# Gate weights laid over the query and key weights, first activations over the queries' staging buffer, and a new order of steps in a two-layer block

## The chip, the cores and the metric

The kernel runs on one core of a Trainium2 chip. The core has five engines with a queue of instructions each: TensorE (PE in the profile; its weight loads stand apart as PEld), VectorE (DVE), ScalarE (ACT), GpSimd (POOL) and SyncE (SP), which here issues all DMA transfers. The metric is the time of one execution on the device in microseconds (us). Of several executions the median counts.

## The reference

The input x has 2048 rows of 512 values in float32. The block is an attention layer followed by a gated feed-forward layer, each behind a layer norm and with its input added to its output:

```python
h  = x + A_ref(layernorm(x), wqkv, wo)
h2 = h + B_ref(layernorm(h), w_gate, w_up, w_down)
```

`A_ref` has 32 heads of 16 values and a sliding window: a row looks at itself and at the 255 rows before it. `B_ref` is `(sigmoid(x @ w_gate) * (x @ w_up)) @ w_down` with 1376 inner columns.

## The kernel before, in words

**Numbers.** Products that need float32 accuracy are made from float16 pieces: each operand is split into a high and a low half, and three multiplications (high by high, high by low, low by high) are added up in the accumulator (`mm3`, L360, and its like in `do_group` and `do_mix`). So every weight and every activation passes through a scaling (its largest magnitude is found first: `prep`, `do_amax`, `scale`), a copy that gives the high half and a subtraction that gives the low half.

**First half.** The rows are taken in 8 blocks of 256. For a block, `do_ln` normalizes two tiles of 128 rows and transposes them into `xT`; `do_qk` makes queries and keys from the first two thirds of the weight tile `W1`, and `do_v` makes the values from its last third. Queries go through a staging buffer, `sq0` (`sq1` for block 1), and three DMA copies for each of four parts (`do_queries`) into the tile from which scores are made; keys go through memory (`do_keys`). `do_s` (L635) makes scores for the row maxima, which DVE takes; `do_m` hands the maxima, through a transpose, to the query tile; `do_st` (L680) makes the transposed scores, which ACT exponentiates and POOL masks; `do_pv` multiplies them with the values, `do_o` and `do_wo` bring the result back into rows and project it. The step numbers run through the blocks: s0 to s7 belong to block 0, s56 to s63 to block 7.

**Second half.** The first four tiles of rows are taken one by one: `do_ln2` normalizes and transposes them into `X2`, `do_early` and `do_gu` multiply them with gate and up weights. The other tiles go in pairs (`do_pair`, L1000), and `do_group` multiplies a pair with seven products of halves instead of eight, for which sums and differences of weight halves are kept as well (`do_T`, L945, for gate and up; `do_sums`, L1257, for the down weights). For the last four pairs the down product is folded in the same way (`do_mat` makes seven operands A11, S1, S2, A12, S3, S4, A22 and transposes them by DMA; `do_mix` multiplies them; mix0 to mix3). The remaining tiles go through `do_down`.

**Storage.** Tiles live in pools. The pool `qkv` on the left holds `W1`, `sq0`, `xT` and small tiles. Once the last block's queries, keys, values and query copies are done, `open_x2` (L1542) closes it and opens the pool `x2p` in its place with the high and low halves of the gate weights (`Wg`), the first third of the up weights (`W0u`), the sums of the gate weights (`Tg`) and the four tiles of `X2`. `do_T` for the gate weights loads its pieces into rows 8 to 11 of X, which must have been stashed to memory by then (`vacant0`, `vacant1`).

**Order.** Each piece of work is a generator whose `yield`s name a price, the keys that it needs, and buffers that it takes from a ring. The order of the steps is not worked out in the kernel: `TABLE` (L65) lists all 4458 of them, such as `s0.1`, `prep0/a` or `qk0*4`; a letter behind the slash is the engine where there is a choice (a ACT, v DVE, g POOL). `Order.step` (L267) takes the next step of the named piece and emits its instructions. Each engine, and the DMA queue of SP, runs its own instructions in the order of the list and waits by semaphores for the others. The prices in the `yield`s take no part when the kernel runs; only the program that made the list used them.

```python
def step(self, name, choice):
    piece, (costs, needs, *rest) = self.live[name]
    ...
    self.on = {"v": DVE_, "a": ACT_, "g": POOL_}[choice] if choice else next(iter(costs))
    ...
        self.live[name][1] = piece.send(((0.0, self.on), *places))
```

The functions that the change touches, and what calls them:

Of the kernel before, what the change touches and what calls it, by code (L numbers as in the profile page):

```python
# [69 lines left out]
prep2/v warm0 warm5 load_x6 load_x4 prep1 prep2/v ln3 prep1 prep2/g ln3/v warm7 qk4*4 prep1 prep1/v prep1 prep2/v prep3/v prep2/v prep2/g qk4*3 prep3/v  # L70
prep3/a prep2/a prep3/a prep2/a prep2/g prep2/a*2 prep3 qk4 qk5 qk4/a qk5*4 qk4 ln6 qk5*3 ln5 prep2/g fill0 fill2 ln4/g qk5/a prep1/a prep3 warm6 v2*2 qk5
v2*2 prep1 queries2 queries1 queries3*2 queries1 queries3 queries1 queries0 load_x7 queries0*2 queries6 queries7 queries4 amax2 v0 prep1/v v0 prep1 prep1/a
v2/a v0*2 qk3*3 prep1 prep3 ln7 v0/a queries5 amax1 amax0 queries7 queries5 queries4 qk2 qk3*3 qk2 qk3*2 prep3/a amax2/v amax3 queries2 qk3/a qk2*2 qk3 qk2*4
v1*3 fill0 fill1 qk2/v qk2 prep3/v fill0 prep3/g keys0*2 v1 qk7*3 prep3/v qk7 v1/a qk7*2 qk6 amax1/v ln8 amax3/v prep3/a ln5/a qk6 qk7*2 qk6 ln7 ln6 fill2
prep3/g prep3/v prep3/a amax0/a prep3/g qk6*5 warm8 amax4 queries4 keys0 ln9 qk7/v qk7 v3*2 qk6/v qk6 ln4 v3*2 ln4/v ln5/a queries2 amax4/a v3/a ln5/v prep3/a
s0*2 fill2*2 ln6/a s0 s0.0 s0.1 s0.2 s0*2 s0.3 v4 s0.4 s0*2 s1 ln5 s0.5 s0.6 s1 s1.0 s1.1 s0 v4 s0.7 ln10 ln5/a ln6/a s2 v4 s1 queries7 queries6 amax7
queries6 keys1*2 queries5 amax5 amax6 keys0 s1 s2.0 s1.2 v4 s1.3 s1*2 s1.4 s1 s1.5 s1 s1.6 s2 s1.7 fill2 ln6/g amax7/a v4/a qk8 ln7/a s2 s2.1 qk8 s2.2 s2*2
qk8 s2.3 s2.4 s2 qk8*3 s3*2 s2.5 s3 qk8 ln11 qk8 s3.0 s3.1 s3.2 open_work0 s2 qk9 s3 s2.6 s3.3 s2 qk9 s2.7 s3 qk9 s3.4 s3 qk9 s3 qk9 s3 qk8/a qk8 amax5/a
keys1 amax8 qk9 fill1 ln8 qk9*2 s3.5 s3.6 s3.7 qk9/a s4 qk10 s4.0 m0*2 s4*2 qk10 s4.1 s4 s4.2 s4.3 qk10 s4 s4.4 qk9 qk10 s4 s4.5 s5*2 qk10*4 qk11 s5.0 s5.1 m0
keys1 s5 qk11 s5 qk11*2 s4 s5.2 s4 amax6/a qk10/a prep3/a qk10 s5.3 qk11 s4.6 qk11 s5*2 s4.7 qk11 s5.4 s5.5 s6 qk11 s6.0 s5 s6 qk11/a s5 s5.6 st0*2 ln6 s6.1  # L80
s5.7 s6 st0.0 st0.1 s6 st0 ln7/a s6.2 st0 s6 s6.3 s6 st0.2 qk11 prep3/g ln9 ln11 ln7/g st0.3 s6 st0 ln6/a st0 keys2 amax9 keys2 s6.5 s6.6 v5 s6.4 amax8/v
st0.5 s7*2 s6 ln7 s7.0 s7.1 st0.6 s6.7 s7*2 st1 s7.2 s7 st1.0 s7.3 st1 v5 st1.1 s7.4 ln8/v st1 s7*2 st1 s7 st1.2 s7.5 s7.6 st1.3 s8 ln7/a s7.7 st0.4 st1.4
fill1 st0.7 st1*2 s8 s8.0 m1 s8.1 s8 v5 st1.5 s8.2 st1.6 s8 pv0 st2 s8 s8.3 v5 st2.0 m1 s8.4 st1.7 ln8/a st2 s8 s9 st2 s8 pv0 ln8/g st2.1 v5/a st2.2 s8.5 s8.6
s9.0 ln12 ln9/a ln8 st2 s8 st2 st2.3 s9 qk14 s8.7 st2.5 ln10 st2.4 st2 st2.6 st2.7 s9.1 s9*2 s9.2 qk14 s9 st3 qk14 s9.3 pv0/a st3.0 s9.4 st3 s9 queries8 m1
keys2 queries8 qk14 s10 s9.5 st3.1 st3 s9 s10.0 st3 st3.2 qk14 st3.3 s9.6 s9 st3 ln9/a s9.7 s10 st3.4 st3 s10 qk15 st3.5 s10.1 ln9/g s10 qk14 pv0 s10.2 s10.3
st3.6 st4 qk14 s10 st4.0 st4 ln9 qk14 st4.1 st4 qk15 s10 ln13 st3.7 st4.2 s11 st4 pv1 st4 st4.3 qk14/a st4.5 queries9 amax11 o0 pv1 st4.4 ln10/v s10.4 s10.5
s11 s11.0 pv1/a st4 queries8 amax10 queries9*2 s10 s11.1 st5 s11 st4.6 s10.6 s11 qk15 s11.2 st5.0 st4.7 st5 s11 ln10/a s11.3 s11.4 s11 st5 qk15 st5.1 ln10/g
s11 st5.2 s11.5 st5 s11 s11.6 st5 st5.3 s10 s11.7 st5.5 st5 st5.4 qk15*2 s12*2 st6 s10.7 st5.6 st6.0 qk15*2 st6*2 pv2 s12 queries10 m2 pv1 st5.7 m2 ln11/a
qk14 s12.1 s12.0 s12.2 pv2 o1 qk15/a st6.1 st6.2 s12 pv2/a st6 s12 st6 s12 s12.3 m2 st6.3 s12.4 st6.5 st6 s12.5 s13 s12 st6.6 s13.0 st7 queries10 s12 s12.6
st7.0 st7 queries10 s13 s12.7 st7 st7.1 s13 st7.2 s13.1 st7 s13 st7 st7.3 st7.5 s13 st7 s13.2 pv2 st8 s13 s13.3 s13 pv3 queries11 st7.6 s13.4 queries11 st8.0  # L90
ln12 o0/g st6.4 s13.5 st8 s14 queries11 s13.6 st7.4 st6.7 st7.7 o2 st8.1 st8 s13 s14.0 s14 ln14 s13.7 s14.1 st8 s14 pv3 st8.3 st8.2 s14.2 s14 pv3/a st8 s14
st8 s15 s14.3 qk15 s14.4 st8.6 qk12 st8.7 qk12 st9 s14 qk12 s15.0 pv3 st9.0 s14 st9 qk12 st8.4 o1/g o2/g st8.5 s14.5 st9.1 st9 s15 s14.6 qk12 s15 st9 st9.2
keys3 o3 s15.1 s15 s15.2 qk12 st9 st9.3 s15 s15.3 st9.6 s15.4 st9.5 st9.4 st8.8 qk12 s14 st9 s15 s16 st10 s14.7 st9.7 qk13 s15 qk13 s15.5 s16 st10 s16.0 s15
st10.0 s15.6 s16.1 st10 qk13 pv4 st10.1 o3/g st9.8 s16 qk12 st10 s16 s15.7 s16.2 wo0 st10.2 m3 wo1 qk12/a s17 st10 s16 s16.4 m3 pv4 wo1/g s16.3 s17.0 qk12
st10.6 st10.3 wo1/a m3 st10 pv4/v s16 st11 s17 st10.7 wo1/g ln14 s16.5 s16 qk13 st11.0 wo1 s17.1 st11 qk13 s16 s16.6 st11.1 st11 s16.7 s17 qk13 st11.2 s17.2
st11 s17*2 st11.3 st11 s17 s17.3 qk13 s17.4 st11.6 st11 s17.5 s17 keys2 keys3 st11.7 s17.6 qk13 s17 st12 s18*2 s17.7 ln13 st10.5 st10.4 st11.4 st12.0 s18.0
st12 pv5 wo1 st12.1 s18.1 st12 s18*3 st12 pv4 st12.2 s18.2 wo1 o4 st10.8 st11.5 st11.8 wo0/g s18.3 st12.3 s18.4 s18 st12 s18 st12 s18.5 s18 pv5 s18.7 s18.6
# [1631 lines left out]
```

## Time and profile before

| | us |
|---|---|
| median of 3 runs | 768.06 |
| lowest and highest | 763.97, 768.09 |
| profiled execution | 765.89 |
| its span in the trace | 764.0 |
| PE busy | 734.1 |
| DVE busy | 630.1 |
| ACT busy | 442.8 |
| POOL busy | 337.6 |

The span runs from the first to the last instruction that the profile shows; 1.9 us of the profiled execution lie around it. Busy times are sums over the instructions of an engine; multiplications on PE overlap, and their ends are modelled. A row of a group of instructions reads: line, engine, operation, what it writes and reads, shapes, count, then busy time and mean duration in ns, then the engine's idle time just ahead of them and what ended it. In a table by stages, columns are the engines' busy times, the granted clock of PE, the DMA engines' share and their rate. A row of the timeline gives start and duration in us, engine, line, operation and, in brackets, how long the engine was idle before it and what it waited for.

### The profile page before, as it was taken

The page shows a single profiled execution, that of the slowest core. Times are in us where ns is not written, and L with a number is a line of the kernel's source. Part 1 is how long each engine was busy: PE and PEld are TensorE (multiplying, and loading weights), DVE is VectorE, ACT ScalarE, POOL GpSimd, SP SyncE. Part 2 cuts the span into 40 slices and gives each one's busy share as a digit, 9 for nine tenths or more (in the row PEclk, how much of TensorE's full clock was granted, in tenths as well). Part 3 has the DMA queues.
Part 4 walks back from the last instruction along what each step waited for, and adds up shares of the span by engine and source line. Part 5 has one row for each costly group of instructions (what it writes and reads, how often), then busy time and mean ns, then how long its engine had stood idle before and what let it go on. Part 6 is the DMA issues. An engine that isn't in the chain of part 4 may idle for free.

```text
span 764.0 us, 18698 instructions
## 1 busy us (share of the span) xinstructions
PE 734.1 (96%) x6930; PEld 486.5 (64%) x6930; DVE 630.1 (82%) x1887; ACT 442.8 (58%) x770; POOL 337.6 (44%) x418
## 2 busy tenths in 40 slices
PE   3999999999999999999998899999999899999998
PEld 3777777777777677786765444454544654757473
DVE  6989999988779888697879989976999769596752
ACT  5745888787777778787778966621442224122320
POOL 7653557554553545366547611132330326441620
PEclk9999999999999999999999999999999999999999
DMA  9783463665976655366746658532656754645463
GB/s 316 238 263 100 120 151 67 163 145 116 172 149 152 126 89 116 91 81 142 111 98 139 173 135 250 129 64 59 142 144 143 135 104 85 102 114 88 93 101 83
DMA packets 182395, 100.97 MB, mean 132 GB/s; under 512 B 153440, under 2 KB 159584, under 8 KB 182304
## 3 DMA queue, kind: packets, MB, share of 16 engines
q1 hardware_dynamic: 182304, 99.78, 59.7%
q8 instruction: 54, 0.88, 0.5%
q14 instruction: 37, 0.30, 0.2%
HBM read 37.36 MB, written 13.11 MB: 66 GB/s over the span
## 4 chain that ended last, share of the span: by engine, by line
PE 73%; DVE 12%; DMA 7%; ACT 4%; issue 3%; SPq 1%; DVEq 0%; ACTq 0%
PE mmp L363 23%; PE pvp L747 9%; PE sp L1095 8%; PE sp L659 8%; PE stp L1095 5%; PE stp L721 3%; PE stp L711 3%; PE stp L363 2%; PE pvp L1095 2%; PE sp L1367 2%; PE stp L710 2%; PE stp L712 2%; PE stp L1367 1%; PE sp L363 1%; DVE junk L646 1%
## 5 line engine op out<-in xcount | busy, mean ns | idle before, releaser
L646 DVE CUSTOM_DVE_ANT_0 junk<-sp,mask 128x320 bf16<-128x320 f32 (+4 forms) x512 | 215.0, 466 | 32.4 <-PE sp L659 29.4
L688 ACT ACTIVATE pa<-stp,kappa 128x512 f32<-128x512 f32 (+1 forms) x256 | 157.3, 646 | 40.8 <-PE stp L712 35.5
L659 PE MATMUL sp<-SK,SQ 96*128 96x256 f16 (+3 forms) x960 | 127.6, 232 | 2.9 <-DMA SK<-mem 1.2
L1095 PEld LDWEIGHTS <-SQ 128*128 128x128 f16 x756 | 73.8, 98 | 73.0 <-issue 1.6
L363 PE MATMUL mmp<-xT,W 128*128 128x256 f16 x768 | 109.8, 272 | 1.8 <-ACT xT L316 1.6
L688 ACT ACTIVATE pb<-stp,kappa 128x512 f32<-128x512 f32 x128 | 84.7, 686 | 19.9 <-PE stp L721 18.4
L659 PEld LDWEIGHTS <-SQ 96*128 96x128 f16 x960 | 79.1, 97 | 26.3 <-issue 8.6
L694 POOL TENSOR_SCALAR_AFFINE_SELECT pa<-pa 128x1024 f32<-128x1024 f32 x56 | 63.0, 1128 | 34.0 <-ACT pa L688 34.0
L363 PEld LDWEIGHTS <-W 128*128 128x128 f16 x768 | 70.0, 97 | 12.5 <-issue 4.1
L699 POOL TENSOR_SCALAR_AFFINE_SELECT pa<-pa 128x512 f32<-128x512 f32 x64 | 42.8, 669 | 62.6 <-ACT pa L688 60.3
L747 PE MATMUL pvp<-pa,VT 128*17 128x128 f32 (+1 forms) x1408 | 62.5, 307 | 0.0
L711 PE MATMUL stp<-SQ,SK 100*128 100x256 f16 x224 | 59.9, 270 | 0.0
L699 POOL TENSOR_SCALAR_AFFINE_SELECT pb<-pb 128x512 f32<-128x512 f32 x64 | 42.3, 667 | 33.5 <-ACT pb L688 33.4
L712 PE MATMUL stp<-SQ,SK 100*128 100x128 f16 x256 | 55.4, 218 | 0.2 <-ACT pb L688 0.2
L710 PE MATMUL stp<-SQ,SK 100*128 100x128 f16 x224 | 49.3, 220 | 3.6 <-ACT pa L688 2.6
L747 PEld LDWEIGHTS pvp<-pa,VT 128*17 128x17 f32 x1408 | 37.7, 97 | 22.8 <-issue 2.2
L363 PE MATMUL mmp<-WO,oT 128*128 128x512 f16 x192 | 50.6, 379 | 0.9 <-DMA oT<-whl 0.9
L363 PE MATMUL mmp<-W,xT 128*128 128x512 f16 x192 | 49.5, 379 | 0.0
L721 PE MATMUL stp<-SQ,SK 100*128 100x256 f16 x256 | 47.4, 272 | 1.4 <-ACT pa L688 1.3
L363 PE MATMUL mmp<-WD,hT 128*128 128x512 f16 (+1 forms) x204 | 48.6, 379 | 0.0
L363 PEld LDWEIGHTS <-x 128*128 128x128 f16 x288 | 27.9, 98 | 28.7 <-issue 1.8
L646 DVE DVE_READ_ACCUMULATOR2_ANT mq<- 128x1 f32 x512 | 42.5, 83 | 0.0
(371 smaller groups left out, 1471.3 us busy)
## 6 DMA issues: line engine op xcount, KB each, us to landing
SQ<-sq SPq DMA_DIRECT2D x96, 128.0 KB
SK<-mem SPq DMA_DIRECT2D x16, 384.0 KB
chunk<-in_wd_dram SPq DMA_DIRECT2D x20, 256.0 KB
mem<-sk SPq DMA_DIRECT2D x8, 512.0 KB
...
```

What stands on the lines that cost most here:

```text
L363: PE.matmul(ps, a_of(a, k), b_of(b, k), start=(k == 0 and i == 0), stop=(k == n - 1 and i == 2))
L646: V.tensor_tensor_reduce(out=junk[:, c0:], in0=ps[:, c0:], in1=mask[:, c0:], scale=1.0, scalar=-3.0e38, op0=ALU.add, op1=ALU.max, accum_ou ...
L659: PE.matmul(ps[:, col:col + k1 - k0], q, SK[0:96, (2 * a + hf) % 5, 4 * (p % 2) + j, k0:k1], start=True, stop=True)
L688: S.activation(dst, a, AF.Exp, scale=kappa)
L694: G.affine_select(out=f, in_=f, pattern=[[0, 8], [-1, 128]], compare_op=ALU.is_gt, fill=0.0, base=0, channel_multiplier=1)
L699: G.affine_select(out=p, in_=p, pattern=[[0, 4], [1, 128]], compare_op=ALU.is_ge, fill=0.0, base=0, channel_multiplier=-1)
L710: PE.matmul(a[:, 0:128], ks(k0, g, j), qs(b, g, j, 0, 128), start=True, stop=True)
L711: PE.matmul(a[:, 128:384], ks(k0 + 1, g, j), qs(b, g, j, 0, 256), start=True, stop=True)
L712: PE.matmul(a[:, 384:512], ks(k0 + 3, g, j), qs(b, g, j, 128, 256), start=True, stop=True)
L721: PE.matmul(a[:, u, :], ks(k0 + 2, g, j + u), qs(b, g, j + u, 0, 256), start=True, stop=True)
L747: PE.matmul(ps[32 * j:32 * j + 17, u, q0:q1], VT[:, kt % 6, 8 * j + g, :], w[:, j, c:c + q1 - q0], start=first, stop=last, skip_group_chec ...
L1095: PE.matmul(out, x7[p][0][:, kk, MATS[a], ha, :], mv, start=first and i == 0, stop=i == 5, skip_group_check=True)
```

## The change

The query and key parts of `W1` become a tile of the pool `keep`, which lives throughout; the value part becomes a tile of its own, `W1v`, in the old pool. `sq0` moves to `keep` as well. The gate weights' halves are then written over `W1`, and the four tiles of `X2` are laid over `sq0`. `open_x2` opens only `W0u` and `Tg`. Two steps without work are added: `open_wg` says that `W1` is free (all of block 7's query and key products are done), `open_sq` that `sq0` is free (its query copies are done). The steps that used to wait for `open_x2` wait for the one that concerns them: loads and halves of the gate weights for the first, the normalized rows of `do_ln2` for the second. The folded gate weights, which lie in `Tg`, still wait for `open_x2`.

Some prices are altered, and `TABLE` is replaced as a whole; it has 4460 steps. The number and shapes of the products on PE stay. Some steps change their engine.

```diff
 TABLE = """
-load_x0 load_x1 load_w1 load_w2 load_w0 load_w3 zeros0 ln0 load_w14 load_x3 load_w9 load_w8 ln1 prep0/a ln0 ln1 prep0/v ln0/v prep0/v ln0/v prep0/a ln0/g
+load_w0 load_x0 load_w3 load_x1 load_w1 load_w2 zeros0 load_x3 load_w4 load_x2 load_w14 load_w10 load_w9 load_w15 load_w11 ln0*2 prep0/a*2 ln1 prep0/a ln0/v
+load_w8 load_w12 load_x4 load_w5 load_w13 load_w6 load_x6 load_w7 ln1 prep0/v ln0/a prep0 ln1/a ln0/g prep0*2 ln4 ln1/a ln0 ln1/g zeros1 fill0 fill1 ln0/v
+warm2 prep1/a prep0/a prep0 prep0/a prep0 prep0/a ln1 warm1 prep0 prep0/a ln1/a ln4 prep0 ln2 prep2/a qk0 ln2 qk1 qk0 prep2/a qk0 warm3 qk0 ln3 prep2/a ln5
...
+    W1 = keep.tile([P, 2, KT, 2 * D], F16, name="W1")
+    sq0 = keep.tile([P, 2, 4, 4, 2, 64], F16, name="sq0")
...
-    W1 = qk.tile([P, 2, KT, 3 * D], F16, name="W1")
+    W1v = qk.tile([P, 2, KT, D], F16, name="W1v")
...
-        e, nx = yield alt("xn", DVE_, DVE=0.46, ACT=0.61), [e], [rings[0]]
+        e, nx = yield alt("xn", DVE_, DVE=0.46, ACT=0.61), [e, *late], [rings[0]]
...
-        e, nt = yield {DMA_: 1.295}, [e], ["mt"], 0.2, 0.7
+        e, nt = yield {DMA_: 1.13}, [e], ["mt"], 0.2, 0.7
...
-        yield {DVE_: 0.0}, ["x2p", ("wo", t), ("stash", 6), ("stash", 7)]
-        e, n = yield from layernorm(t, ("wo", t), x2p, ("xn2", "hl2"), dst, [], ["x2"])
+        e, = yield {DVE_: 0.0}, ["sq free", ("stash", 6), ("stash", 7)]
+        e, n = yield from layernorm(t, ("wo", t), x2p, ("xn2", "hl2"), dst, [], ["x2"], [e])
...
-        e, nF = yield {DMA_: 0.475}, ["x2p" if early else "p2", ("scale", nm)], [ring], n / 300
+        e, nF = yield {DMA_: 0.475}, ["wg" if early else "p2", ("scale", nm)], [ring], n / 300
...
-        e, = yield {POOL_: 4 * (n * 0.0021 + 0.15), DVE_: 4 * (n / 960 + 0.08)}, ends
+        e, = yield {POOL_: 4 * (n * 0.0021 + 0.15), DVE_: 4 * (n / 960 + 0.163)}, ends
...
-        e, = yield {ACT_: 4 * n / 1200 + 0.187, DVE_: 4 * n / 1920 + 0.12}, [e]
+        e, = yield {ACT_: 4 * n / 1200 + 0.187, DVE_: 4 * n / 1920 + 0.12}, [e] + (["x2p"] if early else [])
...
-            e, *r = yield {DMA_: 1.295}, [e], [] if kk else ["x7"], 2.45
+            e, *r = yield {DMA_: 1.52}, [e], [] if kk else ["x7"], 2.45
...
-        e, = yield {POOL_: 2.76, DVE_: 1.4}, [e]
+        e, = yield {POOL_: 2.76, DVE_: 1.72}, [e]
...
-        wg4 = x2p.tile([P, 2, KT, 2, 512], F16, name="Wg", bufs=1)
-        for c in range(2):
-            W["g", c] = wg4[:, :, :, c]
         W["u", 0] = x2p.tile([P, 2, KT, 512], F16, name="W0u", bufs=1)
         T["g"] = x2p.tile([P, 4, 2, 2, 512], F16, name="Tg", bufs=1)
-        X2.extend(x2p.tile([P, 2 * KT, P], F16, name=f"x2{i}", bufs=1) for i in range(NP))
         plan.mark("x2p", e)
+
+    def open_wg():
+
+        e, = yield {DVE_: 0.0}, [("qk", NB - 1, c, j) for c in range(2) for j in range(2)]
+        for c in range(2):
+            W["g", c] = W1[:, :, :, c * D:(c + 1) * D]
+        plan.mark("wg", e)
+
+    def open_sq():
+
+        e, = yield {DVE_: 0.0}, [("copied", NB - 1, 0)]
+        flat = sq0.rearrange("p h j i u t -> p (h j i u t)")
+        X2.extend(flat[:, 1024 * i:1024 * i + 1024].rearrange("p (m q) -> p m q", m=2 * KT) for i in range(NP))
+        plan.mark("sq free", e)
```

More of the change, by code (lines that the diff above doesn't have):

```diff
@@ L70 @@
[L70 to L97, printed above, removed]
@@ L170 @@
-v15 s63.6 st58.0 st57.4 st57.8 stash2 st58 pv28 s63 st58.1 st58 v15 s63.7 st58.2 st58 v15 m15 wo13/v st58.3 wo13/v vacant0 st58 m15 v15/a st58.5 st58.4 wo12/g
-st58 amax23 pv28 open_x20 st58.7 st58.6 wo13 vacant1 ln22 ln20*2 ln21 ln20 ln21 ln22 T0 st59 m15 st59 ln21 st58.8 ln22 st59.0 st59.1 st59 T0 wo13 st59 wo12/a
-st59.2 wo13 st59.3 ln20/v*2 pv28/v wo12/v ln23 ln20/v T1*2 split2 st59 st59.6 st59 st59.7 st59.5 ln23 ln20 st59.8 pv29 st60 st60.0 st60 st60.1 wo13 st60 wo13
-st60 ln21/v st59.4 T0/a pv28 T0 T0/a st60.2 T0 st60.3 wo13 st60.5 st60 amax34 st60 pv29 T0/v T1/a T1 T1/a st60.6 ln21/a st60.7 T1 ln21/v T0/a st61 wo12 o28
@@ new lines @@
+pv27 s63.1 wo8 st57.0 st57 wo8 st57.1 s63 st57 o27 vacant1 ln21 st56.8 st56.5 o26/g st56.4 st57.2 st57.3 s63.2 s63.3 ln23 wo8*2 st57.4 st57 s63 st57.6 s63
+st57 s63 v15 st58 s63.4 s63 pv28 v15 st57.7 stash2 s63.5 o27/v s63.7 ln22 wo13 s63.6 st58.0 st57.8 st57.5 st58 st58.1 st58 v15 st58.2 st58 v15 st58.3 vacant0
+st58*2 amax23 wo13/v m15 wo13/v ln20 v15/a st58.5 wo13/v wo12 ln20 st58.7 st58.6 pv28 wo12/g m15 wo13 ln22 ln20 ln20/a T0*2 st59*2 st59.0 ln22 st58.8 st58.4
+st59.1 st59 m15 st59 st59.2 st59 wo13 st59.3 wo12/a pv28/v open_x20 pv28 T1*2 o28 st59.6 st59 wo13 st59.7 st59.5 st59.4 T0/a st60 st60.0 st59.8 ln20/v*2
@@ new lines @@
+group8.7 group8.6*2 group9.4 pair4/v group8.7 group9.4 mat8 mix0.11 mat10 mat7 group8.5 group10.0/a group9.3/v mat11/v group10 group9.5 group8.5 group9
+group10.1 mix1 group10 pair4 group8.6/a group9.6 mix1.1 mat13/a mat9/a mat13/g mat13 mat9/v mat11/v group8.5 group9.7 group8.6/v group8.5/a group10.2/a mix1
+group10 group8.5/g mat11/g group10.3/g pair4 group10.5 mat9 mix1 group8.5 mix1 mix1.3/a mix1.0/a group9.6 mix1 group8.6 mix1 group10 mat12 pair4/g pair4/a
+group9.5 group9.7 mat11 mix1.4/g mix1.6 mix1.5 group10.6 mix1.1 pair4/v mix1 mix1.6 group10.5 pair4 mix1.7 group10.4 group11 mix1*2 mix1.8 mix1.5 mix1*2
@@ L231 @@
+group17.7*2 group17.5 mix3.12 down7 down6*2 group17.5 group17.7 group17.5 group17.5/v*2 group17.5 down7 down6*3 down7*4
 """
@@ L405, in tile_block @@
     for i, pool in enumerate((qk, wp)):
-        stage[i] = pool.tile([P, 2, 4, 4, 2, 64], F16, name=f"sq{i}"), pool.tile([P, 2, 4, B], F16, name=f"sk{i}")
+        stage[i] = pool.tile([P, 2, 4, 4, 2, 64], F16, name=f"sq{i}") if i else sq0, pool.tile([P, 2, 4, B], F16, name=f"sk{i}")
     wsrc = {}
@@ L463, in prep @@
         i = "qkvo".index(nm)
-        half = [WO[:, h] if nm == "o" else W1[:, h, :, i * D:(i + 1) * D] for h in range(2)]
+        half = [WO[:, h] if nm == "o" else W1v[:, h] if nm == "v" else W1[:, h, :, i * D:(i + 1) * D] for h in range(2)]
         am = small.tile([P, KT + 1], F32, name="am")
@@ L489, in prep, with layernorm @@
         plan.mark(("prep", nm), t)
-    def layernorm(t, key, pool, rings, dst, after, more=()):
+    def layernorm(t, key, pool, rings, dst, after, more=(), late=()):
         e, n = yield {DVE_: 1.0}, [key], ["ln"]
@@ L1625, in last_exp @@
         plan.mark("last exp", e)
-    for piece in (open_work, open_x2, open_p2, open_rest, last_exp, retire):
+    for piece in (open_work, open_wg, open_sq, open_x2, open_p2, open_rest, last_exp, retire):
         plan.add(piece())
```

286 lines of the change are left out of this document (153 added, 133 removed).

## The prediction

> **What bounds the kernel now.** I read the page first: its busy shares and its chain of waits.
>
> ```profile
> span 764.0 us, 18698 instructions
> PE 734.1 (96%) x6930; PEld 486.5 (64%) x6930; DVE 630.1 (82%) x1887; ACT 442.8 (58%) x770; POOL 337.6 (44%) x418
> PE 73%; DVE 12%; DMA 7%; ACT 4%; issue 3%; SPq 1%; DVEq 0%; ACTq 0%
> ```
>
> TensorE (PE) is the bound, and its multiplications are the same before and after, in number and shape. What the change can win is time in which PE runs below its rate, so the first question is how much of that there is. The busy row leaves 764.0 − 734.1 = 29.9 us. That is a lower bound, as the next two rows show, the first from the chain in order of time, the second from the groups of instructions:
>
> ```profile
> 748.55 11.67 PE mmp L363 x54
> ...
> L363 PE MATMUL mmp<-WD,hT 128*128 128x512 f16 x180 | 43.6, 379 | 0.0
> ```
>
> Fifty-four multiplications of 512 columns follow one another in 11.67 us, 216 ns each, while one of them is 379 ns long in the record. A wait of up to 163 ns between two of them therefore shows as busy time, and the true loss is somewhat above 29.9 us. The Trainium skill (Perfetto Trace Analysis, section Identifying the Most-Contended Engine) states this as a rule: matmul busy time is a bad metric, because matmuls are pipelined. The trace agrees (216 against 379 ns); by the rule the 4% that the page leaves understates what there is to win, by the busy row it is all.
>
> Next I asked where the loss lies, with a table by stage (columns: PE, PE loads, DVE, ACT, POOL busy, granted clock, DMA share, GB/s):
>
> ```profile
> 0.00:14.00 14.00, 4.14 (x34) 3.98 (x35) 8.04 (x24) 6.45 (x12) 10.16 (x23) 1.00 0.85 290
> 14.00:33.00 19.00, 16.27 (x171) 14.09 (x170) 17.78 (x45) 16.81 (x35) 10.94 (x16) 1.00 0.90 297
> ...
> 53.00:113.00 60.00, 57.63 (x623) 43.69 (x622) 58.18 (x285) 46.84 (x96) 27.87 (x41) 1.00 0.54 140
> 113.00:400.00 287.00, 285.63 (x3735) 214.64 (x3733) 242.04 (x929) 221.43 (x373) 152.31 (x196) 1.00 0.62 120
> 400.00:445.00 45.00, 39.47 (x446) 22.83 (x445) 40.38 (x86) 39.34 (x65) 27.00 (x31) 1.00 0.66 149
> 445.00:590.00 145.00, 144.14 (x719) 70.01 (x718) 127.82 (x254) 60.02 (x97) 33.67 (x38) 1.00 0.57 134
> 590.00:615.00 25.00, 21.65 (x161) 15.18 (x159) 18.37 (x47) 6.24 (x11) 5.84 (x6) 1.00 0.80 148
> 615.00:764.00 149.00, 145.21 (x903) 87.86 (x900) 100.71 (x191) 38.79 (x72) 55.14 (x52) 1.00 0.50 94
> ```
>
> The losses are 14.00 − 4.14 = 9.9 us at the start, 2.7 behind it, 2.4 in the first attention stage, 1.4 in 287 us of attention, 5.5 in the passage from attention to the second half (400 to 445), 0.9, 3.4 at 590 to 615, and 3.8 at the end, which is the tail behind PE's last product. The clock is 1.00 throughout. Four places can move: start, first attention stage, passage, and 590 to 615. The last two, 8.9 us together, are where the change could act most directly.
>
> **The change part by part.** The sum is made against the profiled execution, 765.89 us with a span of 764.0; the median of the three runs is 768.06, 2.2 us above it.
>
> Storage. The moved tiles cost no instruction. Two steps of no work are new, `open_wg` (all of the last block's query and key products done) and `open_sq` (its query rows copied out), and the gate weights and the first tiles' activations wait for these instead of for everything that `open_x2` names. A write into the old W1 must follow the last block's projections on PE, and a transpose into sq0 the last query copies on the same DMA queue; in the new list both stand far behind them, so I count no new wait. The gain would be gate weights that start earlier. The list does not take it: T0's two loads, the first of the gate weights' folded pieces, stand in both versions behind `vacant0` or `vacant1`, because the loads land in rows of X that must first be stashed to memory, and the first weight copy of T0 on ACT stands only two exponentials earlier (behind st59.7 instead of st60.1). So I take zero for the storage itself, and read the rest from the order.
>
> Start. New order of loads: w0 x0 w3 x1 w1 w2 instead of x0 x1 w1 w2 w0 w3. These rows show what follows now:
>
> ```profile
> 8.14 0.63 ACT L328 ACTIVATE W<-wq 128x512 f16<-128x512 f32 x1 [6.06 <-DMA wq<-in_wqkv_dram]
> 8.68 0.19 ACT L328 ACTIVATION_READ_ACCUMULATOR W<-wq 128x1 f32 x1
> 8.80 0.63 ACT L328 ACTIVATE W<-wq 128x512 f16<-128x512 f32 x1
> ...
> 9.43 0.80 ACT L509 ACTIVATE chunk<-X,nb,rs 128x512 f32<-128x512 f32 x1
> 9.56 0.16 DVE L472 TENSOR_REDUCE am<-am 128x1 f32<-128x4 f32 x1 [1.57 <-ACT W L328]
> ...
> 10.26 0.63 ACT L316 ACTIVATE RT<-chunk 128x512 f16<-128x512 f32 x1
> ...
> 11.56 1.34 ACT L316 ACTIVATE W<-wq,sq 128x512 f16<-128x512 f32 x2 [0.66 <-DVE sq L349]
> ...
> 14.63 1.00 ACT L316 ACTIVATE xT<-mmp 128x1024 f16<-128x1024 f16 x1
> ...
> 15.69 5.40 PE L363 MATMUL mmp<-xT,W 128*128 128x256 f16 x48 [1.65 <-ACT xT L316]
> ```
>
> The fifth load is there at 8.14 and the sixth by 8.80. In the new list ACT takes the maxima of w0, w1 and w2, and w1 and w2 are the fifth and sixth: 8.14 + 2 × 0.82 = 9.78, where the reduction over the four maxima starts at 9.56 now. Then ACT does the first tile's high half (0.63), the second tile's normalization and high half (0.80 + 0.63), one maximum of wk (0.82), four weight copies (2 × 1.34) and the transposed activations (1.00): 9.78 + 6.56 = 16.3, where PE starts at 15.69 now. Term: +0.6 us. ACT loses the 0.66 of waiting and gains the tile on which DVE worked. Bounds −1 (the loads land sooner) and +2 (the second tile's products come late as well).
>
> First attention stage. DVE is busy for 58.18 of 60 us, so the stage goes by DVE. Ahead of st4's first product the new list has 155 DVE steps instead of 160, ahead of st12's 231 instead of 233. Those that are gone stand later. Term 0, bounds −2 and +2.
>
> Passage. What PE waits for there, and what a layer norm and a fold of gate weights cost DVE:
>
> ```profile
> PE stp L710 <- ACT pa L688: 2.6, 5, 1.3
> PE stp L721 <- ACT pa L688: 1.1, 2, 0.9
> PE mmp L363 <- DMA oT<-whl: 0.9, 1, 0.9
> ...
> 411.04 0.93 DVE L511 TENSOR_SCALAR X<-X,mv,rs 128x512 f32<-128x512 f32 x1
> ...
> 414.14 0.69 DVE L496 BATCH_NORM_STATS2 st<-X 128x6 f32<-128x512 f32 x1
> 414.86 0.18 DVE L498 BATCH_NORM_AGGREGATE mv<-st 128x2 f32<-128x6 f32 x1
> 415.08 0.15 DVE L500 TENSOR_SCALAR rs<-mv 128x1 f32<-128x1 f32 x1
> ...
> 461.15 1.79 DVE L984 TENSOR_TENSOR F<-F 128x256 f32<-128x256 f32 x4
> ```
>
> ACT and DVE are busy for 39.34 and 40.38 of 45 us, and the exponentials come late because both engines also do weights and layer norms. The new list takes the statistics of tile 1 (0.69 + 0.18 + 0.15 = 1.02 us) ahead of the tight stretch, those of tile 0 a little ahead, and gives tile 0's normalization (0.93) from DVE to ACT. That relieves DVE by 2 × 1.02 + 0.93 = 3.0 us and adds about 0.8 to ACT, which is just as short. The waits on ACT in the rows sum to 3.7 us. I take 2.0 of the stage's 5.5. Bounds: −5, all but a trace of it, and +1.5, because only three steps of PE, nine multiplications of 216 ns (1.9 us), now stand between the transpose of tile 3's activations and its first reader, where twelve steps stood.
>
> Second half. What holds PE at 590 to 615:
>
> ```profile
> 584.56 1.80 DVE L1269 TENSOR_TENSOR OS<-OS 128x256 f32<-128x256 f32 x4
> ...
> 592.10 1.05 PE L1095 MATMUL stp<-Tb,SQ 128*128 128x352 f16 x6 [1.35 <-DVE X L1114]
> ...
> 593.79 1.52 SPq L1049 DMA_TRANSPOSE SQ<-OS  x1
> ...
> 601.71 1.16 PE L1380 MATMUL mmp<-WD,hT 128*128 128x256 f16 x9 [0.45 <-DMA hT<-X]
> ...
> 606.24 1.49 PE L1367 MATMUL sp<-F,RT 128*128 128x256 f16 x12 [1.08 <-DMA RT<-X]
> ...
> 608.09 1.48 PE L1367 MATMUL sp<-WD,RT 128*128 128x256 f16 x12 [0.36 <-DMA RT<-X]
> ```
>
> 1.35 + 0.45 + 1.08 + 0.36 = 3.2 of the 3.4 us are these four waits, all in or just ahead of mix0. In the constants that the diff changes, the four subtractions of a sum go from 1.4 to 1.72 (the row has 1.80, and 1.79 for the gate's kind) and the pair's transpose from 1.295 to 1.52 (the row has 1.52): the new order was laid out with the prices that these rows show, at the very steps that run late here. In it the transposes of mix0's first three products stand 12 to 14 PE steps ahead of their readers instead of 2 to 4, and S4's 5 instead of 0. I let 2.5 of the 3.2 us go. Bounds −3.4, and +5 for new waits of this kind elsewhere (rivals). Two more of the folded sums, eight subtractions, go from DVE to POOL:
>
> ```profile
> L699 POOL TENSOR_SCALAR_AFFINE_SELECT pb<-pb 128x512 f32<-128x512 f32 x64 | 42.3, 667 | 33.5 <-ACT pb L688 33.4
> ...
> 403.34 1.00 DVE L791 TENSOR_TENSOR OS<-OS,rc 128x512 f32<-128x512 f32 x1
> 403.76 1.08 POOL L699 TENSOR_SCALAR_AFFINE_SELECT pb<-pb 128x512 f32<-128x512 f32 x1
> ```
>
> Here a DVE instruction with two operands in SBUF and a POOL instruction overlap, and POOL's took 1.08 us where the mean is 667 ns: 0.41 more. Eight such meetings are 3.3 us, in a stage (445 to 590) where DVE has 17 us and POOL 111 us free; so 0, and +3.3 if that cover is gone. The Trainium skill (SBUF — State Buffer, on the shared port pair) speaks against such a move: the pair is an exclusive lock, and the loser fully blocks. The two rows agree; by the rule the sum would be at most those 3.3 us higher.
>
> Sum: 0.6 + 0 − 2.0 − 2.5 + 0 = −3.9, and 765.9 − 3.9 = 762.0 for an execution like the profiled one. Runs of before lie up to 2.2 above that one, so I take 763 for the median.
>
> **The rivals.**
> Nothing moves (766 to 768): ACT and DVE hold the passage, the gate loads stand where they stood, and what goes at mix0 comes back in another mix. For it: near-equal lists, T0 unmoved. Against it: the four named waits.
> Much goes: passage and mix0 are both cleared, 765.9 − 5.0 − 3.4 = 757.5; with one more us from the DVE-bound stage 756.5. For it: both are queueing, not work. Against it: in the passage two engines are near 90% busy.
> Slower: transposes late in the mixes. In the list no PE step stands between a transpose and its reader at 8 places after (three in mix1 as before, one more there, one in mix2, three in mix3) and at 5 before. The whole latency of one is in the chain of waits:
>
> ```profile
> 582.06 3.86 DMA hT<-X
> ```
>
> If the three new ones in mix3 each bare it, that is 3 × 3.86 = 11.6 us, 765.9 + 0.6 + 11.6 = 778. It decides as soon as PE is fewer than three products of about 1.3 us behind its list there. Against it: of the five such places before, one shows a wait, and 0.36 us long.
>
> **How the numbers follow.** A measurement of this kernel tells about 1% from no change: with a median of 768, below 760.4 or above 775.7. The forecast has 0.47, nothing moves 0.25, much goes 0.20, slower 0.08. Faster by over 1%: all of "much goes" and 0.04 of the forecast's lower side, 0.24. Slower: 0.08. Within 1%: 0.68. The range reaches down into "much goes", 756, and up through "nothing moves" with one or two new waits, 771.
>
> **What would show it.** The first long run of 48 projections at about 16.3 instead of 15.69; PE's idle in the stage before the first sigmoid table load at 3 to 4 us instead of 5.5; no waits of mix0 on transposes; PE's total idle near 26 us. It would be wrong if PE waits for transposes in mix1 to mix3, for tile 3's activations in the passage, or if the gap at the passage is as wide as before.

## The result, and the profile after

| | before | after |
|---|---|---|
| median, us | 767.14 (4 runs, 763.97 to 768.09) | 758.36 (4 runs, 758.12 to 759.06) |
| profiled execution, us | 765.89 | 758.37 |
| its span, us | 764.0 | 756.0 |
| PE busy, us | 734.1 | 732.3 |

The ratio of after to before is 0.9894, with a 95% interval of 0.9863 to 0.9926: faster by 1.06%. The forecast was 763 in a range of 756 to 771; "much goes" had named 756.5 to 757.5.

The page of after, its span, busy shares and chain of waits:

```profile
span 756.0 us, 18726 instructions
PE 732.3 (97%) x6930; PEld 486.6 (64%) x6930; DVE 622.5 (82%) x1863; ACT 447.5 (59%) x784; POOL 336.3 (44%) x431
PE 83%; DVE 6%; ACT 3%; issue 3%; DMA 3%; POOL 1%; SPq 0%; DVEq 0%; ACTq 0%; POOLq 0%
```

The chain now runs through PE for 83% of the span instead of 73%. PE's idle time fell from 29.9 to 23.7 us, which is 6.2 of the 8.0 us. The other 1.8 left the busy row itself, with the same 6930 products: waits of less than a product's length had stood there as busy time. The table by stage of after, in the columns of the prediction's:

```profile
0.00:14.00 14.00, 3.88 (x34) 3.47 (x35) 7.67 (x23) 8.39 (x17) 10.03 (x23) 1.00 0.88 302
14.00:33.00 19.00, 16.64 (x172) 14.36 (x172) 17.27 (x44) 17.26 (x35) 13.77 (x18) 1.00 0.84 253
...
53.00:113.00 60.00, 58.16 (x634) 44.56 (x632) 57.82 (x290) 47.45 (x96) 30.65 (x44) 1.00 0.60 142
113.00:400.00 287.00, 286.85 (x3745) 215.22 (x3743) 244.13 (x935) 222.57 (x374) 151.95 (x197) 1.00 0.57 123
400.00:445.00 45.00, 40.79 (x444) 23.18 (x443) 42.61 (x90) 39.71 (x64) 22.83 (x28) 1.00 0.66 150
445.00:590.00 145.00, 144.25 (x736) 71.73 (x735) 124.53 (x245) 62.99 (x105) 35.94 (x44) 1.00 0.59 138
590.00:615.00 25.00, 24.49 (x162) 15.47 (x160) 16.03 (x33) 5.30 (x9) 6.59 (x12) 1.00 0.68 134
```

PE's idle time went from 3.4 to 0.5 us at 590 to 615, from 5.5 to 4.2 in the passage, from 1.4 to 0.15 in the 287 us of attention, from 2.4 to 1.8 in the first attention stage. At the start it is 10.1 instead of 9.9.

These windows are fixed in time, while after runs ahead of before by more and more, so the same window holds other work. For the experiments I therefore use a measure that does not shift. The 54 products in the prediction show 216 ns for 512 columns, 0.42 ns a column; with such prices (the float32 products with the values by their own spacing, 64 in 2.72 us) PE's products have about 706 us of work of their own in every kernel here. For each product, its start less the work ahead of it is PE's lag. What the lag grows by over a stretch of PE's own work is what PE lost there, hidden waits included; the start is counted from the span's first instruction. The prices are those at full clock, so a lower clock counts as loss too. All runs, in us:

```
PE work from to   0-50  50-100 100-185 185-190 190-200 200-360 360-370 370-420 420-500 500-580 580-705
old list of steps
 before          18.33   7.66    4.09    1.32    0.41    5.34    0.52    9.66    0.88    4.69    0.92
 storage_only    19.21   7.68    4.09    0.98    0.38    5.23    0.52    9.81    0.87    3.84    0.88
 passage_new     17.48   7.66    4.09    1.30    1.69    5.22    0.59    7.31    1.16    3.82    0.93
 second_new      18.41   7.67    4.09    1.31    2.54    5.22    0.59    7.31    0.42    2.35    0.86
 mix_new         18.22   7.67    4.09    1.34    0.45    5.22    0.52    9.30    0.80    2.95    0.85
 keys_new        19.19   7.74    8.03    0.09    0.36    5.23    0.52    9.79    0.86    4.20    0.85
 relief_alone    17.42   7.67    4.09    1.31    1.87    5.34    0.52   12.48    0.89    3.92    0.85
 pv27_dve        17.80   8.14    4.08    1.30    0.57    5.23    0.52   10.18    0.86    4.58    0.93
new list of steps
 after           17.87   6.96    3.82    0.09    0.37    5.16    0.59    7.31    0.46    2.40    0.85
 order_only      19.60   6.98    3.80    0.09    0.37    5.18    0.59    7.31    0.55    2.63    0.85
 relief_undone   17.76   6.97    3.82    0.09    0.37    5.16    0.59   12.38    0.53    2.42    0.89
 pv27_act        19.00   6.95    3.80    0.09    0.37    5.16    0.59    7.30    0.42    2.66    0.86
 sums_on_dve     19.40   6.97    3.82    0.09    0.37    5.65    0.59    7.31    1.79    2.50    0.85
 pool_sums       17.83   6.96    3.82    0.09    0.37    5.16    0.59   11.74    1.31    2.66    0.85
```

Two things in this table are the clock's and not the order's. The first is the start. The trace's record of PE's granted clock begins 12.8 to 14.4 us into the span in eight executions (17.4 to 18.3 in the first column) and at 17.5 to 18.7 us in five, and in keys_new it is 0.50 once more until 19.1 us (18.4 to 19.6 in these six). Until then products stand about twice as far apart as later, although the table by stage shows 1.00 for want of a record. The same first twelve projections, in after and in order_only:

```profile
14.88 1.47 PE L362 MATMUL mmp<-xT,W 128*128 128x256 f16 x12 [1.40 <-ACT xT L315]
```

```profile
14.98 2.71 PE L371 MATMUL mmp<-xT,W 128*128 128x256 f16 x12 [0.93 <-ACT xT L324]
```

The second is a stretch at a granted clock of 0.50 in the middle of four executions: keys_new (200.0 to 203.4 us), relief_alone (412.6 to 416.0), relief_undone (420.6 to 427.4) and pool_sums (420.5 to 427.3). By my estimate from the prices above, PE did 1.8, 1.7, 2.8 and 2.6 us of its own work in them; at twice the price, that much of their lag, at most, is the clock's. PE had stood just ahead of each, or stood as it began: 2.0 us, 0.6 and 1.1, 2.7, 2.7. In before and after, where PE's longest wait behind the start is 1.3 and 0.6 us, there is no such stretch, and in second_new a wait of 2.1 us brought none; where the limit lies, no run shows.

From before to after the lag falls by 7.9 us: 0.5 at the start, 0.7 in the first attention stage (50 to 100), 0.3 behind it, 1.2 at the keys of one block (185 to 190), 2.35 in the passage (370 to 420), 0.4 behind it, 2.3 around mix0 (500 to 580), 0.2 elsewhere.

What PE waits for, over the whole execution (total, times, longest), before:

```profile
PE stp L710 <- ACT pa L688: 2.6, 5, 1.3
...
PE stp L1095 <- DVE X L1114: 1.3, 1, 1.3
...
PE sp L659 <- DMA SK<-mem: 1.2, 1, 1.2
...
PE sp L659 <- DVE mq L646: 0.9, 2, 0.7
```

and after:

```profile
PE stp L711 <- ACT pa L689: 2.3, 7, 0.6
...
PE stp L1096 <- DVE chunk L1115: 0.6, 2, 0.4
PE sp L1368 <- DMA RT<-X: 0.5, 1, 0.5
...
PE sp L660 <- DVE mq L647: 0.2, 1, 0.2
```

The wait for the keys (`SK<-mem`) is gone. That for the row maxima (`mq`), 0.9 us at the first attention stage, is 0.2. Of the four waits at mix0, 3.2 us together, two are left: 0.4 us for DVE (one of the two for `chunk`), just ahead of mix0, and 0.5 us for a transpose (`RT<-X`).

### The profile page after: what moved, and what is told of

The parts are those of the page before. It is cut to its first block, busy times and chain, and to the rows that moved or that the text cites. A ratio compares the mean times of both kernels' runs of the same rounds, so it can differ in the third digit from the quotient of the medians.

```text
span 756.0 us, 18726 instructions
## 1 busy us (share of the span) xinstructions
PE 732.3 (97%) x6930; PEld 486.6 (64%) x6930; DVE 622.5 (82%) x1863; ACT 447.5 (59%) x784; POOL 336.3 (44%) x431
## 4 chain that ended last, share of the span: by engine, by line
PE 83%; DVE 6%; ACT 3%; issue 3%; DMA 3%; POOL 1%; SPq 0%; DVEq 0%; ACTq 0%; POOLq 0%
PE mmp L362 25%; PE pvp L748 10%; PE sp L1096 9%; PE sp L660 8%; PE stp L1096 6%; PE sp L362 5%; PE stp L722 3%; PE stp L712 3%; PE stp L362 2%; PE pvp L1096 2%; PE sp L1368 2%; PE stp L711 2%; PE stp L713 2%; PE stp L1368 1%; ACT pa L689 1%
## 5 line engine op out<-in xcount | busy, mean ns | idle before, releaser
L660 PE MATMUL sp<-SK,SQ 96*128 96x64 f16 (+3 forms) x960 | 127.6, 232 | 1.4 <-DVE mq L647 0.2
L362 PEld LDWEIGHTS <-W 128*128 128x128 f16 x768 | 69.9, 97 | 10.8 <-issue 2.0
L362 PE MATMUL mmp<-W1v,xT 128*128 128x512 f16 x192 | 50.1, 378 | 0.0
L362 PEld LDWEIGHTS <-sq 128*128 128x128 f16 x288 | 27.9, 98 | 27.0 <-issue 0.4
L362 PE MATMUL mmp<-WD,hT 128*128 128x512 f16 (+1 forms) x192 | 44.4, 379 | 0.0
```

Of the source, the lines that this page charges most:

```text
L362: PE.matmul(ps, a_of(a, k), b_of(b, k), start=(k == 0 and i == 0), stop=(k == n - 1 and i == 2))
L660: PE.matmul(ps[:, col:col + k1 - k0], q, SK[0:96, (2 * a + hf) % 5, 4 * (p % 2) + j, k0:k1], start=True, stop=True)
```

## The experiments

"Old list" and "new list" are the `TABLE`s of before and after. Where no other edit is shown, the old list runs on the new storage.

**Storage alone.**

```diff
-wo12/g st58 amax23 pv28 open_x2 st58.7 st58.6 wo13
+wo12/g st58 amax23 pv28 open_wg open_sq open_x2 st58.7 st58.6 wo13
```

(old list, in the kernel of after)

> The new storage with the old list of steps; the two steps without work stand directly ahead of open_x2. Theory (the order gives the whole gain, the storage none): same time as before, ratio 0.998 to 1.002, and PE's waits at the passage, at keys and at mix0 are all back. Rival (the storage itself lets work start earlier, or spares waits): part of the 8 us is there, ratio 0.993 to 0.997, with the passage (400 to 445 us) near 4 us of idle instead of 5.5.

Measured: 765.75 us, ratio 0.9994 (0.9974 to 1.0015). The new storage alone is worth nothing that can be measured.

**Order alone.** The new list on the storage of before; steps that would have waited for `open_x2` wait for it only where they write into that pool.

```diff
-        yield {DVE_: 0.0}, ["x2p", ("wo", t), ("stash", 6), ("stash", 7)]
+        yield {DVE_: 0.0}, [("wo", t), ("stash", 6), ("stash", 7)]
...
-        e, nF = yield {DMA_: 0.475}, ["x2p" if early else "p2", ("scale", nm)], [ring], n / 300
+        e, nF = yield {DMA_: 0.475}, ([] if early else ["p2"]) + [("scale", nm)], [ring], n / 300
```

> The new list of steps on the old storage. Only the bookkeeping is relaxed so that the list can be taken as it stands: the loads of the gate pieces into X and the statistics of the first tiles no longer name the opening of the pool, which their data do not touch; the halves of the gate weights and the first tiles' activations are written into the pool that open_x2 opens. Theory (order alone): 758 us, ratio 0.988 to 0.991, as the whole change. Rival (the storage is needed for the passage): 2 to 3 us of the gain are missing, ratio 0.992 to 0.994, all of it between 370 and 450 us of the span.

Measured: 759.11 us, ratio 0.9905 (0.987 to 0.9941). The whole gain comes from the order, and the old storage can carry it. Its span is 2.1 us above that of after; its lag is 1.7 above in the first 50 us of work, where its clock comes late, and within 0.25 in every other stretch.

**The second half of the order.** The old list up to 361 us of PE's work, then the steps that are left, as the new list orders them.

```diff
 ... st56 s62 wo8 st56 s62 pv27
-st56.3 st56.6 wo10 s62.7 s62.6 s62.5
+stash0 open_sq o26 o25/g ln2 s62.6 stash5 st56.6
```

> New storage; the old list up to the 361st us of PE's work (just before the passage), the new one behind it. From the two traces, PE's lag behind its own work differs by 2.8 us up to there and by 7.9 us at the end, so theory (the stages' gains add up): 5.1 us faster than before, ratio 0.992 to 0.995. Rival (the later stages only carry on what was gained earlier, or an old first half spoils the new second half): under 2 us, ratio 0.997 to 1.0.

Measured: 761.85 us, ratio 0.9935 (0.9912 to 0.9959). The passage's lag is that of after, 7.31, and mix0's too, 2.35. The stages' gains add up. In this run, in passage_new and in relief_alone PE also loses 1.3 to 2.1 us at 190 to 200, in a place where the list is the old one in all of them: a wait for a masking step on POOL that the other executions do not show.

**The passage alone.** As above, but back to the old list at 430 us of PE's work.

> New storage; the old list, except that the steps between the 361st and the 430th us of PE's work stand as in the new one. Theory (the passage's own order is worth what the two traces show there): 2.1 to 2.7 us faster than before, ratio 0.996 to 0.998, with mix0's waits of 3.2 us still there. Rival (the passage is bound by the sum of ACT and DVE work, and the gain came from a DVE that arrived earlier): no gain, ratio 0.999 to 1.001, and 5.5 us of idle at 400 to 445 us.

Measured: 763.2 us, ratio 0.9964 (0.9945 to 0.9983); the lag of the passage 7.31 against 9.66. The gain belongs to the order in this stretch, and nothing ahead of it or behind it is needed.

**mix0 alone.** The new list from 510 to 560 us of PE's work.

```diff
 ... group1.7/a group2.5 group3.0/a sums0/v sums0 group3
-group3 group4 group1.4 pair2 sums1 sums1
+group1.6 group1.7/g pair2 sums1 sums1 group3 group2.5 group1.4
```

> New storage; the old list, except that the steps between the 510th and the 560th us of PE's work (down products ahead of mix0, and the first part of mix0) stand as in the new one. Theory (local order): PE's lag behind its own work grows by about 2.4 us between 500 and 580 us of work instead of 3.8 to 4.7, 1.4 to 2.3 us faster than before, ratio 0.997 to 0.9985. Rival (the gain at mix0 comes from DVE work that went to POOL further ahead): lag over that stretch 3.6 us or more, ratio 0.999 to 1.001.

Measured: 764.6 us, ratio 0.9981 (0.9965 to 0.9997); lag 2.95 from 500 to 580, where the old list has 3.8 to 4.7 (mean 4.2) in six executions and the new list 2.4 to 2.7 (mean 2.5) in its six. Most of the gain is local. The DMA queue of before and of after at this place (start, time on the queue):

```profile
581.16 0.33 SPq L1261 DMA_DIRECT2D OS<-in_wd_dram  x1
...
586.28 2.64 SPq L1336 DMA_TRANSPOSE hT<-X  x2
588.96 0.58 SPq L1515 DMA_DIRECT2D out_dram<-WO  x1
589.99 1.24 SPq L1336 DMA_TRANSPOSE hT<-X  x1
...
601.29 2.64 SPq L1336 DMA_TRANSPOSE RT<-X  x2
```

```profile
573.94 0.34 SPq L1262 DMA_DIRECT2D OS<-in_wd_dram  x1
...
578.93 5.40 SPq L1337 DMA_TRANSPOSE hT<-X  x4
...
595.64 3.43 SPq L1337 DMA_TRANSPOSE RT<-X  x2
```

In after four of mix0's transposes go out together behind the load of the sums, and the last of them ends on the queue at 584.3; mix0's first long run of products starts at 587.1. Before, the fourth ended at 591.2, and that run started at 593.0.

**The sums' engines.** The new list with the folded sums on the engines they had before.

```diff
-... T7/v ... T11/g ... T10/g ... T8/g ...
+... T7/g ... T11/v ... T10/v ... T8/v ...
```

(the letters of these pieces' subtractions alone)

> The whole change, with the engines of the folded sums as they were before: that of the seventh on GpSimd, the eighth, tenth and eleventh on VectorE. This puts the relief of VectorE ahead of mix0 back. Theory (mix0 gains by the order at its own place, by transposes issued earlier): the loss between 500 and 580 us of TensorE's work stays at 2.4 us, within 0.5; time within 0.7 us of the change. Rival (the relief of VectorE makes its transposes early): 3.5 us or more.

Measured: 760.5 us, ratio 0.9923 (0.9894 to 0.9952). mix0's lag stays at 2.50, as my theory had it. The time was expected within 0.7 us of after and is 2.1 above it. The profiled execution's span is 3.5 us longer: 1.5 comes from the start, where its clock comes late, 0.5 from 200 to 360, ahead of the altered steps, and 1.3 from 420 to 500. In this last stretch the move to POOL (twelve subtractions there, four back to DVE, eight net), which I had counted at nothing, does win about a microsecond, as far as one execution of each kernel tells.

**The keys.** The new list from 165 to 200 us of PE's work.

```diff
 ... s30.0 ln12/v s29.6 qk17 s29.5 pv10
-amax25 m6 o9 st22.6 amax22/a amax26
+amax22/v amax26 o9 m6 wo2 ln12/v st22.6 st22.7
```

> New storage; the old list, except that the steps between the 165th and the 200th us of PE's work (around the query and key copies of block 4) stand as in the new one. Theory (PE waited for keys because twelve query copies of 128 KB started 3 us later ahead of them on the same queue): PE's lag between 185 and 190 us of work falls from 1.0 to 1.3 us to 0.1, ratio 0.998 to 0.999. Rival (the landing depends on other traffic): the wait for keys stays, ratio 0.9995 to 1.0005.

Measured: 769.09 us, ratio 1.003 (1.0016 to 1.0045). The wait for the keys is gone, 0.09 in place of 1.3, but the seam between the lists makes a new one ahead of it: 8.03 us of lag from 100 to 185 instead of 4.09. Of the 3.9 us between them, 2.0 are one wait for a row maximum and up to 1.8 the half clock that followed it. My expectation of the time missed, since I had not reckoned with the seam. PE's waits for row maxima in this kernel (total, times, longest):

```profile
PE sp L670 <- DVE mq L657: 2.8, 3, 2.0
```

PE now comes to the keys 3.9 us later, while they are asked back only 1.5 us later than in before (at 212.56 us against 211.04). So this run does not tell whether the local order or PE's delay took the wait away. What the whole new order does for the keys is seen in the DMA queue, of before and of after:

```profile
193.46 8.20 SPq L610 DMA_DIRECT2D SQ<-sq  x12
...
202.91 0.33 SPq L596 DMA_DIRECT2D mem<-sk  x1
...
211.04 0.33 SPq L601 DMA_DIRECT2D SK<-mem  x1
```

```profile
190.46 5.83 SPq L611 DMA_DIRECT2D SQ<-sq  x7
...
197.13 3.02 SPq L611 DMA_DIRECT2D SQ<-sq  x5
...
201.12 0.33 SPq L597 DMA_DIRECT2D mem<-sk  x1
...
207.19 0.37 SPq L602 DMA_DIRECT2D SK<-mem  x1
```

The keys come back from memory 8.1 us after they were sent in before, 6.1 us in after; the twelve query copies begin 3.0 us earlier, of which 1.4 is what after is ahead by then. That the keys come back 3.9 us earlier, and PE comes to them only 1.4 us earlier, is why the wait is gone; which steps do it was not taken apart.

**The relief of VectorE in the passage, undone and alone.** The prediction put the passage's gain down to 3.0 us taken off DVE: the statistics of tiles 0 and 1 made earlier, tile 0 normalized on ACT. One kernel is the whole change with the second layer norms' first steps of all four tiles in the order of before:

```diff
-... s62.4 ln21 s62.6 ... m15 wo13/v ln20 v15/a ... m15 wo13 ln22 ln20 ln20/a T0 ...
+... s62.4 s62.6 ... m15 wo13/v v15/a ... pv28/v open_x2 ln22 ln20 ln20 ln21 ln20 ln21 ln22 ln21 ln22 ln20/v ln23 pv28 ... m15 wo13 T0 ...
```

> The whole change, but the statistics of the first four tiles' second layer norm stand again directly behind open_x2, in the old order among themselves, and the first tile's normalization is on DVE again. Theory (the passage is eased because about 3 us of DVE work were taken out of it): the passage gives back 1.5 to 2.3 us, PE's lag over 370 to 420 us of work is 9.0 to 9.7 instead of 7.3, ratio to before 0.9915 to 0.9935. Rival (the order of the other steps of the passage does it): 7.3 to 7.8, ratio 0.989 to 0.991.

The other is the old list with only these moves made:

```diff
-... vacant1 ln22 ln20 ln20 ln21 ln20 ln21 ln22 ... wo13 st59.3 ln20/v ...
+... s63.2 stash0 open_sq ln21 ln21 ln21 stash5 ... v15 m15 ln20 ln20 ln20 wo13/v ... vacant1 ln22 ln22 ... wo13 st59.3 ln20/a ...
```

> New storage and the old list, in which only the layer norms are moved: the statistics of tile 1 about 10 us of PE's work ahead of the passage, those of tile 0 directly ahead of open_x2, and the first tile's normalization on ACT. Theory (DVE relief is the cause): 1.5 to 2.3 us faster than before, lag over 370 to 420 us of work 7.4 to 8.2 instead of 9.7, ratio 0.997 to 0.998. Rival (the rest of the order): lag 9.2 or more, ratio 0.999 to 1.001.

Measured: undone 764.37 us, ratio 0.9975 (0.9961 to 0.9989), lag of the passage 12.38; alone 768.26, ratio 1.0017 (1.0 to 1.0033), lag 12.48. Both kernels lie above both lists (7.31 and 9.66), by 2.7 to 5.2 us. Part of that is the clock. Its stretch at 0.50 in relief_undone, as a row of the table by stage, and six like products, there and in after:

```profile
420.57:427.39 6.82, 6.20 (x24) 3.11 (x23) 6.68 (x12) 4.71 (x8) 2.81 (x3) 0.50 0.80 175
...
423.58 2.77 PE L371 MATMUL mmp<-WO,oT 128*128 128x512 f16 x6
```

```profile
420.12 1.46 PE L362 MATMUL mmp<-WO,oT 128*128 128x512 f16 x6
```

All ten runs of undone have a mean clock of 0.993 to 0.998, those of after 1.000. Of alone's ten, the four at 0.998 or less took 768.4 to 769.4 us, the other six 765.9 to 768.8. Without the clock's share, at most 2.8 and 1.7 us, undone would have a lag of about 9.6, inside the first expectation, and alone about 10.8, still beyond the rival's bound. By this estimate the new list needs these moves: without them its gain in the passage is gone. In the old list they win nothing. DVE's waits of relief_alone in the passage, and PE's of relief_undone:

```profile
DVE X L327 <- ACT X L520: 5.1, 1, 5.1
```

```profile
PE sp L371 <- DVE W L984: 2.7, 1, 2.7
```

In alone, DVE stands for 5.1 us with the high half of tile 0 at the head of its queue, since ACT comes to that tile's normalization only behind exponentials and a copy that waits for a DMA; all of DVE's later work stands behind. In undone, PE stands for 2.7 us for a low half of the gate weights, which DVE makes behind the steps of the layer norms. From the first exponential of step st56 to the last of st63 (391.4 to 440.1 us in before, 388.4 to 434.9 in after), ACT is busy for 41.0 us in before, 40.8 in after, and idle for 7.7 and 5.6. DVE's busy time there falls by 1.4 us, half of the 3.0 that the prediction counted, and its idle time by 0.8. So ACT's work hardly changed, and what it gained is waiting.

**One copy in the passage.** Before, ACT's waits in this stretch (393 to 445 us) were:

```profile
ACT pa L688 <- PE stp L712: 3.7, 6, 1.8
ACT rh L316 <- PE pvp L747: 2.9, 2, 2.0
```

The second is for copies of finished products at the head of ACT's queue, ahead of exponentials. In the new list DVE makes the copy of pv27. I took that letter alone, in both directions:

```diff
-... s63 pv27/a s63.0 pv27 ...
+... s63 pv27/v s63.0 pv27 ...
```

> The old list on the new storage, with one letter altered: the raw copy of the product of block 6's last values (pv27) is made by VectorE instead of ScalarE. In the old list ScalarE stands 2.9 us in two waits for TensorE in front of such copies, with exponentials queued behind. Theory (the passage is lost to in-order queues, and this wait is one large part of it): TensorE's loss between 370 and 420 us of its own work falls from 9.7 us to 8.5 or less, the time by about 1.2 us, ratio about 0.998. Rival (no single wait carries it; another takes its place): 9.2 or more, ratio 0.999 to 1.001.

> The whole change, with the same copy given back to ScalarE. Theory: the loss between 370 and 420 us of TensorE's work rises from 7.3 us to 8.5 or more. Rival (the place of the copy's engine does not matter): 7.8 or less. Time 758 to 760 either way.

Measured: old list with the copy on DVE 766.41 us, ratio 1.0006 (0.9992 to 1.0021), lag 10.18; new list with it on ACT 759.26, ratio 0.9912 (0.9887 to 0.9937), lag 7.30. The rival holds in both: in the first, ACT's waits for scores rise in place of those for `pvp`, which fall from 2.9 to 0.9 us (393 to 447 us):

```profile
ACT pa L699 <- PE stp L723: 6.5, 6, 2.7
...
ACT rh L325 <- PE pvp L758: 0.9, 1, 0.9
```

**More sums on GpSimd.** The new list with the subtractions of the first two folded gate weights on POOL, as a possible better version.

```diff
-T0/v ... T1/v
+T0/g ... T1/g
```

(the letters of the subtractions alone)

> The whole change, with the sums of the first two folded gate weights on GpSimd instead of VectorE (eight subtractions). Theory (work taken off VectorE does not ease the passage or what follows, only waits in the queues do): within 1 us of the change, ratio 0.988 to 0.991. Rival (VectorE's volume is what is short): 1.5 us or more below the change.

Measured: 763.24 us, ratio 0.9968 (0.9955 to 0.998), 4.9 us slower than after; the passage's lag 11.74, of which the half clock is at most 2.6. Neither side expected that. The groups of subtractions of after, where DVE makes all sixteen:

```profile
L985 DVE TENSOR_TENSOR X<-X 128x256 f32<-128x256 f32 x16 | 7.5, 469 | 0.4
```

The same groups in pool_sums, and then ACT's waits there in the passage:

```profile
L994 POOL TENSOR_TENSOR X<-X 128x256 f32<-128x256 f32 x8 | 7.5, 942 | 0.5
L994 DVE TENSOR_TENSOR X<-X 128x256 f32<-128x256 f32 x8 | 4.1, 516 | 0.2
```

```profile
ACT Tg L324 <- POOL X L994: 2.5, 1, 2.5
```

A subtraction takes 942 ns on POOL against 516 on DVE, or 469 in after. ACT, next in its queue, stands for 2.5 us with the copy of the folded weight, and the exponentials stand behind it. PE then stands for 2.7 us for an exponential, and the half clock follows. DVE was relieved of 3.4 us (7.5 less 4.1), and the kernel lost 4.9. Together with relief_alone this shows that taking work off DVE does not by itself ease the passage: what then waits at the head of a queue can cost more than the work taken off.

No kernel beat the change.

## Why the prediction was right or wrong

Right: PE bounds the kernel, its products do not change, and what is won is its lost time. That the idle time of the page is a lower bound on the loss is borne out by PE's busy time, 1.8 us lower with the same products. This agrees with the Trainium skill (Perfetto Trace Analysis, section Identifying the Most-Contended Engine), by which matmul busy time is a bad metric. One reading was wrong: the clock is not 1.00 throughout. In the first 14 us of before the trace has no record of it, and eight products of 128 columns take 1.06 us at 10.42 us and 0.62 at 22.27.

**Storage, 0: right.** storage_only and order_only show it from both sides.

**Start, +0.6: about nothing.** The first run of projections, shown above, begins at 14.88 instead of 16.3. The fifth load was there sooner than the 8.14 us that I took from before, which makes 0.6 of the difference:

```profile
7.58 0.63 ACT L327 ACTIVATE W<-wq 128x512 f16<-128x512 f32 x1 [3.17 <-DMA wq<-in_wqkv_dram]
```

That run is broken off after twelve products, so little of this is won. Over the first 50 us of PE's work, executions with an early clock lose 17.4 to 18.3 us with the old list's start (five, mean 17.85) and 17.8 to 17.9 with the new one (three); with a late clock 18.4 to 19.2 (three) and 19.0 to 19.6 (three). From the spacing of the products I estimate 1.1 to 1.6 us for the half clock in the first group and 2.8 to 3.3 in the second. So the clock moves the start by more than the term, and the 0.5 us between the two profiled executions is within it (1.6 us of half clock in before, 1.1 in after).

**First attention stage, 0: mis-sized by 0.7 us.** The six executions with the new list have 6.95 to 6.98, those with the old 7.66 to 8.14. The wait for row maxima fell from 0.9 to 0.2 us. The step that failed is the counting of DVE's steps ahead of two points: what went is a wait for row maxima, which DVE makes. Which of its steps stood ahead of them I did not take apart.

**Attention, not in the sum: 1.2 us missed.** My table showed 1.4 us of idle in 287 us, and I left it out of the four places that could move. Nearly all of it was one wait, for one block's keys, and the new order, with its copies earlier on the queue, took it away. Whether the local order is enough, keys_new does not show, since PE is late there for another reason.

**Passage, −2.0: the size near (−2.35), the reason only half of it.** The step that failed is taking the relief of DVE by 3.0 us for the cause. DVE's work in the stretch fell by 1.4 us, and the same moves in the old list win nothing: the lag is 2.8 us higher, 1.1 without the clock's share. They are needed all the same: undoing them in the new list costs 5.1 us, at most 2.8 of it by the clock, and the rest is as much as the gain. The 2.0 was a choice out of 5.5, so that the size came near is in part luck. The six executions with the new list's order here, among them one with the copy of pv27 on ACT, have 7.30 to 7.31. So the stretch has to be ordered as a whole, and I found no single step that carries its gain: which of the other moves it takes beside the norms stays open. That tile 3's activations would come too late did not happen.

**Second half, −2.5: right.** The lag fell by 2.3 us between the two profiled executions, and by 1.6 between the means of the old list there (4.18, six executions) and the new one (2.55, six). The reason, transposes and loads earlier on their queue, is borne out by mix_new, which keeps most of it. The rival "slower", transposes late in the mixes, fell: after shows one such wait, of 0.5 us, in the whole second half.

**POOL's sums, 0 with +3.3 as the bound: the sign was wrong.** sums_on_dve shows that they win about 1.3 us at 420 to 500, in one execution of each. The bound's warning came true elsewhere: in pool_sums, where eight more of them stand on a path that ACT waits for.

**The sum.** −3.9 was forecast against the profiled execution, −7.5 was measured. Of the 3.6 missing, 2.2 are the stages counted at nothing (keys 1.2, first attention 0.7, behind it 0.3), 1.1 the start (0.5 of it the clock's), 0.35 the passage, 0.4 what follows it and 0.2 other places, while mix0 gave 0.2 less. That is 4.0 by the lag; the lag fell by 7.9 and the time by 7.5, which takes back the 0.4. I had also added 1 us for the median, as the three runs shown lay above the profiled one. Over all 75 runs of before beside the experiments the median is 766.1, 0.2 above it, so most of that step was the chance of three runs. The case "much goes" had the size, but not the places: its one microsecond from the DVE-bound stage was there (0.7 and 0.3), but passage and mix0 gave 2.35 and 2.3 where it had 5.0 and 3.4, and the keys, which it did not name, gave 1.2.
